# Turning the layer-normed rows by DMA transposes instead of TensorE in the first head of an attention-and-gate kernel

## The chip, the cores and the metric

The kernel runs on one core of one Trainium2 chip. The metric is the device time of the execution in microseconds (us), as the median of several runs.

## The reference

The kernel computes one block of attention with a gated feed-forward branch, in bfloat16. `x` is 2048 rows of 640, normalised per row without a learned scale. There are 32 heads of width 192 with a given key and value cache of 2048 rows, no mask. The feed-forward width F is 1536.

```python
x = A_x
xn = _layernorm(x, axis=-1)                      # (x - mean) / sqrt(var + 1e-5)
q = (xn @ wq).reshape(B, Sq, H, Dh).transpose(0, 2, 1, 3)
scores = jnp.einsum("bhqd,bhkd->bhqk", q, k_cache) * (Dh ** -0.5)
p = _softmax(scores, axis=-1)
o = jnp.einsum("bhqk,bhkd->bhqd", p, v_cache)
s = o.transpose(0, 2, 1, 3).reshape(B, Sq, H * Dh) @ wo
h = _silu(xn @ w1) * (xn @ w3)
return x + s * _silu(h @ w2)
```

## The kernel before

**Layout.** Everything that is multiplied by the weights needs the normalised rows with the 640 features on the partitions. This copy is `xnT`, 128 partitions x 5 chunks x 2048 rows. A second copy, `xnS`, holds the same with the upper and lower 64 partitions exchanged; `swap_rows(qb)` (L298 to L301) makes it for 512 rows with two DMAs from SBUF to SBUF, issued on GpSimd (POOL). Rows go by blocks of 512, `qb` = 0 to 3, and by tiles of 128, 0 to 15.

**Normalising.** `ln_stats(i)` (L179) takes mean and variance of a row tile on VectorE (DVE); for tiles 1 and 4 `ln_sums` does it on ScalarE (ACT). `ln_root(i0)` (L196) turns the variances of two tiles into 1/sqrt on ACT, `ln_scale(i0)` (L214) applies them on DVE. `ln_turn(i0)` (L224) then transposes the two tiles: ten transposes on TensorE (PE) into a PSUM tile of the pool `ps_st`, and two copies to `xnT` on ACT. That pool has two buffers, and the score tiles and the projections use the same two.

**A pair.** The attention of a head goes over four query blocks and, in each, over eight pairs of key tiles. `advance(hd, qb, p, extra)` (L432) does one pair: six score matmuls (L371), one exponential of 128x1024 on ACT (L377), and the value matmuls (L417) of a pair that was scored earlier. `extra` is more PE work, put behind the values. PE runs its instructions strictly in the order in which the program gives them (`pin` keeps that order on each engine).

**Head 0 is special.** While it runs, the rest of `x` is still being normalised, and head 0 and head 1 are projected block by block. `first_project(0, qb + 1)` projects the next block of head 0 (L277, ten matmuls), takes the maxima of the projected rows (L294) and makes the bound `nb` that the exponentials of that block need; `swap_rows(qb + 1)` follows, and `first_project(1, qb)` projects a block of head 1 (L283, twenty matmuls that read `xnT` and `xnS`). Later heads are projected one head ahead. What comes behind which pair is written out by hand in `at`, `extras` and `posts`:

```python
at = (1, 3, 4, 6) if qb else (3, 4, 5, 7)
extras = dict(zip(at, (steps((next_turn, 4 * qb + 4)), steps((next_turn, 4 * qb + 6)),
                       steps((first_project, 0, qb + 1)), steps((first_project, 1, qb)))))
```

so in block 0 the turns stand behind pairs 3 and 4 and the two projections behind pairs 5 and 7, and in blocks 1 and 2 behind pairs 1, 3, 4 and 6. In block 3 only `first_project(1, 3)` is left, behind pair 1.

**Keys.** `load_keys(h)` (L102) issues two DMA transposes (`KA`, `KB`) and the values `vt` on the queue of SyncE (SP). Keys have three buffers, so those of heads 0 to 2 wait for nothing. `copy_keys` (L116) makes a partly exchanged copy `KC` with two copies and a memset on POOL. `key_maxima` (L303) takes maxima of keys on DVE. Before the first pair, `first_bound` makes the bound of block 0 by way of a small matmul, with filler matmuls (`keep_busy`) around it.

After head 0 come 31 heads in the same manner, with feed-forward work between them, and then the output tiles. The change touches none of this.

Of the kernel before, what the change touches and what calls it, by code (L numbers as in the profile page):

```python
# [30 lines left out]
def _kernel_impl(ctx, tc, A_x, A_k_cache, A_v_cache, A_wq, A_wo, B_w1, B_w3, B_w2, out):  # L31
# [54 lines left out]
    def load_weights(h):  # L86
# [12 lines left out]
                keep(nc.gpsimd.dma_start(out=wq[ROWS[t], :, c0:c1], in_=w.rearrange("(s p) d -> p s d", p=DT)))  # L99
        return dict(wq=wq)  # L100

    def load_keys(h, mid=None):  # L102
        kh = A_k_cache[0, h]
        vh = A_v_cache[0, h]
        KA = kvp.tile([P, SK], BF16, tag="KA")
        KB = kvp.tile([P, SK], BF16, tag="KB")
        for K, c in ((KA, 0), (KB, DH - P)):
            for r in ((slice(0, HALF), slice(HALF, SK)) if h == 0 else (slice(0, SK),)):
                nc.sync.dma_start_transpose(out=K[:, r], in_=kh[r, c:c + P])  # L109
            if mid and K is KA:  # L110
                mid()
        vt = kvp.tile([P, NKT, DH + 2], BF16, tag="vt")
        nc.sync.dma_start(out=vt[:, :, 0:DH], in_=vh.rearrange("(t p) d -> p t d", p=P))
        return dict(KA=KA, KB=KB, vt=vt)

    def copy_keys(L, keep=pin):  # L116
        L["KC"] = KC = kvp.tile([P, HALF], BF16, tag="KC", name="KC")
# [10 lines left out]
    with ExitStack() as actx:  # L128
# [30 lines left out]
        x_all = lnx.tile([P, NQT, D], BF16, name="x_all")  # L159

        def load_x(eng, t0, t1):
            eng.dma_start(out=x_all[:, t0:t1, :], in_=x2[t0 * P:t1 * P, :].rearrange("(t p) d -> p t d", p=P))

        load_x(nc.sync, 0, 1)
        load_x(nc.scalar, 1, 2)
# [58 lines left out]
        def ln_turn(i0, copies=(nc.scalar.copy, nc.scalar.copy)):  # L224
            pst = ps_st.tile([P, 2, 1024], BF16, tag="st2", name="pst")
            for t, xn in enumerate(scaled.pop(i0)):
                for c in range(DC):
                    pin(nc.tensor.transpose(out=pst[:, t, c * P:(c + 1) * P], in_=xn[:, c * P:(c + 1) * P], identity=ident_bf[:]))
            return [lambda t=t, cp=cp: pin(cp(out=xnT[:, :, (i0 + t) * P:(i0 + t + 1) * P],
                                              in_=pst[:, t, 0:D].rearrange("p (c q) -> p c q", c=DC)))  # L230
                    for t, cp in enumerate(copies)]

        def next_turn(i0):
            for copy in ln_turn(i0):
                copy()

        keep_busy(15)
        ln_sums(1)
# [17 lines left out]
        def start_head(h):  # L256
            L = loads.pop(h)
            heads[h] = dict(
                h=h, L=L, vt=L["vt"],
                qA=qp.tile([P, SQ], BF16, tag="qA", name="qA"),  # L260
                qF=qfp.tile([P, SQ], BF16, tag="qF", name="qF"),
                qS=qp.tile([P, SQ], BF16, tag="qS", name="qS"),
                qD=qp.tile([DT, SQ], BF16, tag="qD", name="qD"),
                st=stt.tile([P, 4, NQB], F32, tag="st", name="st"),
            )
            pin(nc.vector.memset(heads[h]["st"][:], 0.0))
# [42 lines left out]
        def first_bound():  # L309
# [3 lines left out]
            pin(nc.vector.scalar_tensor_tensor(out=pr[:], in0=hd["st"][:, 0:2, 0], scalar=-SCALE * SLACK,  # L313
                                               in1=hd["st"][:, 2:4, 0], op0=ALU.mult, op1=ALU.mult))
            bp = ps_o.tile([P, 2, 512], F32, tag="ob0", name="bp")
            for t in range(2):
                pin(nc.tensor.matmul(bp[:, 0, 0:1], lhsT=ones_bf[:], rhs=pr[:, t:t + 1], start=(t == 0), stop=(t == 1)))
            nb = stt.tile([P, 1], F32, tag="nbb", name="nbb")
            pin(nc.vector.tensor_copy(out=nb[:], in_=bp[:, 0, 0:1]))
            hd["nb"] = [nb]  # L320
# [83 lines left out]
                late.append(rest)  # L404

        def values(hd, qb, p, pT2):
            vt = hd["vt"]
# [34 lines left out]
        start_head(0)  # L442
        loads[1] = load_weights(1)
        ln_sums(4)
        for s in range(2):
            for k in range(2):
                key_maxima(0, s, k, 2)
        maxima = project_chunk(0, 0, nc.scalar.copy)
        swap_rows(0)
        loads[1].update(load_keys(1))  # L450
        maxima()
        early = [scores(heads[0], 0, p) for p in range(2)]
        keep_busy(2)
        first_bound()
        keep_busy(4)
        ln_stats(5)
        warm = stt.tile([P, 1], F32, tag="warm", name="warm")
        pin(nc.gpsimd.partition_all_reduce(warm[:], heads[0]["nb"][0][:], P, bass_isa.ReduceOp.add))

        start_head(1)  # L460
        all_keys = [(s, k, NQB) for k in range(NQB) for s in range(2)]
        key_slots = list(all_keys)

        def first_project(h, qb):
            maxima = project_chunk(h, qb, nc.vector.tensor_copy if h == 0 else nc.scalar.copy)
            if h == 0:
                maxima()
                next_bound(qb)
            else:
                behind.append(maxima)  # L470

        def steps(*fs):
            return lambda: [f(*a) for f, *a in fs]

        posts = {
            (0, 1): ((ln_root, 4), (ln_stats, 6), (ln_scale, 4), (ln_stats, 7)),
            (0, 3): ((ln_root, 6), (ln_scale, 6), (ln_stats, 8), (ln_stats, 9)),
            (0, 5): ((ln_stats, 10), (ln_stats, 11), (ln_root, 8)),
            (0, 7): ((ln_scale, 8), (ln_root, 10)),
            (1, 2): ((ln_scale, 10), (ln_stats, 12), (ln_stats, 13)),  # L480
            (1, 5): ((ln_stats, 14), (ln_stats, 15), (ln_root, 12)),
            (1, 7): ((ln_scale, 12), (ln_root, 14)),
            (2, 2): ((ln_scale, 14),),
        }
        behind = []
        for qb in range(NQB):
            more = qb + 1 < NQB
            at = (1, 3, 4, 6) if qb else (3, 4, 5, 7)
            extras = dict(zip(at, (steps((next_turn, 4 * qb + 4)), steps((next_turn, 4 * qb + 6)),
                                   steps((first_project, 0, qb + 1)), steps((first_project, 1, qb)))))  # L490
            if not more:
                extras = {1: steps((first_project, 1, qb))}
                loads[2].update(load_weights(2))
                copy_keys(loads[2])
            for p in range(NPAIR):
                advance(heads[0], qb, p, extras.get(p), early.pop(0) if early else None)
# [310 lines left out]
```

## Time and profile before

| | |
|---|---|
| Time, median of 3 runs | 1957.43 us (1957.2 to 1957.73) |
| Span of the profiled execution | 1957.8 us |
| PE busy | 1941.8 us (99%) |
| ACT busy | 1219.9 us (62%) |
| DVE busy | 1137.9 us (58%) |
| POOL busy | 440.5 us (23%) |
| DMA, mean over the span | 78 GB/s |
| First score matmul of head 1 | 89.14 us |

The profiled execution's span, 1957.8 us, is its own time; it lies 0.35 us above the median of the runs. A busy share is that of the whole span. Head 0 with its preparation takes the first 89 us; a line of the timeline has the start and the length in us, engine, source line, operation, output<-input, shape, count, and in brackets the idle time of the engine before it and what ended it.

### The profile page before, as it was taken

Reading aid. Unit: us, or ns where it says so; the run is one execution under the profiler, and the core shown is the slowest. Engines: PE = TensorE matmul, PEld = TensorE weight load, DVE = VectorE, ACT = ScalarE, POOL = GpSimd, SP = SyncE. Lnnn points to the kernel's source line nnn. Section 1 sums busy time; section 2 is a strip of 40 time slices with the busy share of each in tenths; the row PEclk is TensorE's granted clock in tenths of the full one; section 3 lists DMA queues with packets and bytes.
Section 4 is the critical chain, followed back from the end, with each engine's and each line's share of the span. In section 5 each row is a group of like instructions: output and inputs, shape, how many; then the busy total and the mean of one; then the engine's idle time right before and its main releaser. Section 6 shows DMA issues by size and latency. Waiting matters only on the chain.

```text
span 1957.8 us, 60489 instructions
## 1 busy us (share of the span) xinstructions
PE 1941.8 (99%) x27236; PEld 1332.9 (68%) x27236; DVE 1137.9 (58%) x2258; ACT 1219.9 (62%) x1192; POOL 440.5 (23%) x640
## 2 busy tenths in 40 slices
PE   8999999999999999999999999999999999999998
PEld 4676666667766666666666666666666666667776
DVE  6665657676666666666666666666665654531111
ACT  6777767776777777777777777777777777210000
POOL 3422222222222222222222222222222220000000
PEclk8999999999999999999999999999999999999999
DMA  9421313222233332232323232323232112837882
GB/s 183 104 66 42 74 44 74 53 69 59 60 68 63 68 62 68 54 90 68 76 54 76 54 76 46 84 46 84 46 75 44 44 50 75 261 77 139 156 152 56
DMA packets 352906, 153.52 MB, mean 78 GB/s; under 512 B 303792, under 2 KB 345744, under 8 KB 352640
## 3 DMA queue, kind: packets, MB, share of 16 engines
q1 hardware_dynamic: 337200, 117.82, 28.4%
q0 software_dynamic: 8800, 26.55, 5.7%
q10 hardware_dynamic: 6640, 5.21, 1.2%
q8 instruction: 215, 3.52, 0.8%
q14 instruction: 51, 0.42, 0.1%
HBM read 56.23 MB, written 31.98 MB: 45 GB/s over the span
## 4 chain that ended last, share of the span: by engine, by line
PE 97%; DVE 1%; DMA 1%; ACT 0%; POOL 0%; SPq 0%; issue 0%; POOLq 0%; DVEq 0%
PE obank L417 34%; PE st L371 33%; PE ps L283 14%; PE ps_s L630 11%; PE ps_f L649 3%; PE ps_gu L536 2%; DMA KB<-in_A_k_cache_dram 0%; PE ps L277 0%; DMA xnS<-xnT 0%; ACT pT L377 0%; SPq L109 0%; DVE u L541 0%; PE fill L177 0%; ACT t L539 0%; DVE a L543 0%
## 5 line engine op out<-in xcount | busy, mean ns | idle before, releaser
L377 ACT ACTIVATE pT<-st,nb 128x1024 bf16<-128x1024 f32 x1016 | 1130.6, 1114 | 439.8 <-PE st L371 439.1
L417 PEld LDWEIGHTS <-pT 64*128 64x128 bf16 x16384 | 720.9, 94 | 236.1 <-DVE osum L388 0.9
L417 PE MATMUL obank<-vt,pT 64*128 64x193 bf16 x16384 | 856.7, 243 | 0.4 <-DVE osum L388 0.4
L387 DVE COPY osum<-obank 128x386 f32<-128x386 f32 x256 | 142.4, 556 | 513.3 <-PE obank L417 513.3
L371 PE MATMUL st<-qA,KA 64*128 64x512 bf16 x2048 | 394.6, 377 | 3.0 <-ACT pT L377 1.1
L371 PE MATMUL st<-qD,KC 64*128 64x512 bf16 x1024 | 385.6, 377 | 1.9 <-issue 1.8
L371 PE MATMUL st<-qS,KB 64*128 64x512 bf16 x1024 | 385.5, 377 | 0.6 <-POOL qS L289 0.6
L371 PE MATMUL st<-qS,KC 64*128 64x512 bf16 x1024 | 385.6, 377 | 0.1
L371 PE MATMUL st<-qF,KB 64*128 64x512 bf16 x1024 | 385.7, 377 | 0.0
L289 POOL COPY qS<-qA 64x512 bf16<-64x512 bf16 x256 | 193.3, 755 | 598.7 <-DVE qA L285 590.3
L283 PE MATMUL ps<-xnT,wq 64*128 64x512 bf16 x1240 | 288.4, 376 | 0.0
L283 PE MATMUL ps<-xnS,wq 64*128 64x512 bf16 x1240 | 285.9, 376 | 0.1
L371 PEld LDWEIGHTS <-KC 64*128 64x128 bf16 x2048 | 192.1, 94 | 118.3 <-issue 2.0
L630 PE MATMUL ps_s<-wo_sb,oT 128*128 128x320 bf16 (+2 forms) x1536 | 208.8, 299 | 0.0
L371 PEld LDWEIGHTS <-KB 64*128 64x128 bf16 x2048 | 192.8, 94 | 17.8 <-issue 2.9
L283 PEld LDWEIGHTS <-wq 64*128 64x128 bf16 x2480 | 123.7, 94 | 114.0 <-issue 0.4
L630 PEld LDWEIGHTS <-oT 128*128 128x128 bf16 x1536 | 148.3, 98 | 60.5
L394 DVE TENSOR_TENSOR ostage<-osum,rl_all 128x384 bf16<-128x384 f32 x256 | 150.5, 588 | 8.8
L388 DVE TENSOR_TENSOR osum<-osum,obank 128x386 f32<-128x386 f32 x256 | 142.6, 557 | 8.9
L371 PEld LDWEIGHTS <-KA 64*128 64x128 bf16 x2048 | 106.2, 94 | 22.3 <-issue 7.4
L635 DVE SCALAR_TENSOR_TENSOR tmp<-ps_s,g_all 128x320 f32<-128x320 f32 (+2 forms) x32 | 15.6, 487 | 175.8 <-PE ps_s L630 175.8
L99 POOL DMA_DIRECT2D wq<-in_A_wq_dram x62 | 45.5, 733 | 278.0 <-PE ps L283 265.8
(86 smaller groups left out, 1228.4 us busy)
## 6 DMA issues: line engine op xcount, KB each, us to landing
vt<-in_A_v_cache_dram SPq DMA_DIRECT2D x32, 768.0 KB, 6.2
o_scr<-ostage SPq DMA_DIRECT2D x64, 384.0 KB, 3.2
wo_sb<-in_A_wo_dram POOLq DMA_DIRECT2D x1, 7680.0 KB, 32.1
wq<-in_A_wq_dram POOLq DMA_DIRECT2D x31, 160.0 KB, 3.0
hT_scr<-hblk SPq DMA_DIRECT2D x16, 256.0 KB, 2.9
xnS<-xnT POOLq DMA_DIRECT2D x8, 320.0 KB, 6.6
xt<-in_A_x_dram POOLq DMA_DIRECT2D x16, 160.0 KB, 9.2
wq<-in_B_w_dram POOLq DMA_DIRECT2D x31, 80.0 KB, 2.5
```

The costliest lines, as they stand in the source:

```text
L99: keep(nc.gpsimd.dma_start(out=wq[ROWS[t], :, c0:c1], in_=w.rearrange("(s p) d -> p s d", p=DT)))
L283: pin(nc.tensor.matmul(ps[:, t * 512:(t + 1) * 512], lhsT=wq[ROWS[t], s, :], rhs=xs[ROWS[t], s // 2, qs], start=(s == 0), stop=(s == 2 * D ...
L289: keep(nc.gpsimd.tensor_copy(out=qS[ROWS[t], qs], in_=qA[ROWS[1 - t], qs]))
L371: pin(nc.tensor.matmul(st2[:, t * 512:(t + 1) * 512], lhsT=k[ROWS[t], ks], rhs=q[ROWS[t], qs], start=(s == 0), stop=(s == 2)))
L377: pin(nc.scalar.activation(out=pT2[:], in_=st2[:], func=ACT.Exp, scale=SCALE, bias=nb[:]))
L387: pin(nc.vector.tensor_copy(out=osum[:], in_=ov[:, 0, :, 0:DH + 1]))
L388: pin(nc.vector.tensor_tensor(out=osum[:], in0=osum[:], in1=ov[:, 1, :, 0:DH + 1], op=ALU.add))
L394: pin(nc.vector.tensor_tensor(out=ostage[:, b * 2:b * 2 + 2, hg * DH:(hg + 1) * DH], in0=osum[:, :, 0:DH], in1=rl.unsqueeze(2).to_broadcas ...
L417: pin(nc.tensor.matmul(acc["o"][b][:, r, (j % 2) * 256:(j % 2) * 256 + DH + 1], lhsT=pT2[ROWS[r], t * 512 + j * P:t * 512 + (j + 1) * P], ...
L536: pin(nc.tensor.matmul(ps[:, o:o + 512], lhsT=w_sb[:, c, fl * P:(fl + 1) * P], rhs=xnT[:, c, qs], start=(c == 0), stop=(c == DC - 1)))
L630: pin(nc.tensor.matmul(ps, lhsT=oT[:, k, :], rhs=wo_sb[:, k, c0:c1], start=(k == 0), stop=(k == OC - 1)))
L649: pin(nc.tensor.matmul(ps[:, pi * 512:pi * 512 + c1 - c0], lhsT=hT[:, fc, qsl], rhs=w2_sb[:, fc, c0:c1], start=(fc == 0), stop=(fc == FC - ...
```

## The change

Rows 0 to 511 are turned as before. For the other twelve row tiles, `ln_send(i0)` takes the place of `ln_turn`: it scales two tiles and issues one DMA transpose for each on SP, from the scaled tile in SBUF to `xnT`. The statistics, roots, scalings and transposes of the second block (tiles 4 to 7) are placed ahead of the first pair; those of blocks 2 and 3 follow in `posts`. `first_project(0, qb + 1)` stands behind pair 3 and `first_project(1, qb)` behind pair 6 in blocks 0 to 2, and `swap_rows` behind pair 4. The loads of head 1's and head 2's keys on SP come behind the transposes that precede them in program order; `copy_keys` of heads 1 and 2 moves to blocks 2 and 3. The maxima of head 1's projected rows (`behind`) are taken behind pair 3 of block 2 and pairs 3, 5 and 7 of block 3; before, the fourth of them was never taken. The loads of `x` keep their program order.

```diff
+    def load_key(L, h, name):
+        keep = pin if h <= 2 else (lambda x: x)
+        L[name] = K = kvp.tile([P, SK], BF16, tag=name, name=name)
+        c = {"KA": 0, "KB": DH - P}[name]
+        for r in ((slice(0, HALF), slice(HALF, SK)) if h == 0 else (slice(0, SK),)):
+            keep(nc.sync.dma_start_transpose(out=K[:, r], in_=A_k_cache[0, h, r, c:c + P]))
+
+    def load_values(L, h):
...
-        def next_turn(i0):
-            for copy in ln_turn(i0):
-                copy()
+        def ln_send(i0):
+            ln_scale(i0)
+            for t, xn in enumerate(scaled.pop(i0)):
+                pin(nc.sync.dma_start_transpose(out=xnT[:, :, (i0 + t) * P:(i0 + t + 1) * P], in_=xn[:]))
...
         ln_sums(4)
-        for s in range(2):
-            for k in range(2):
-                key_maxima(0, s, k, 2)
+        for k in range(2):
+            key_maxima(0, 0, k, 2)
+        ln_stats(5)
+        ln_stats(6)
+        ln_root(4)
+        for k in range(2):
+            key_maxima(0, 1, k, 2)
         maxima = project_chunk(0, 0, nc.scalar.copy)
         swap_rows(0)
-        loads[1].update(load_keys(1))
         maxima()
+        pr = first_product()
+        ln_stats(7)
+        ln_root(6)
+        ln_send(4)
+        ln_send(6)
+        load_key(loads[1], 1, "KA")
         early = [scores(heads[0], 0, p) for p in range(2)]
         keep_busy(2)
-        first_bound()
+        first_bound(pr)
         keep_busy(4)
-        ln_stats(5)
...
         posts = {
-            (0, 1): ((ln_root, 4), (ln_stats, 6), (ln_scale, 4), (ln_stats, 7)),
-            (0, 3): ((ln_root, 6), (ln_scale, 6), (ln_stats, 8), (ln_stats, 9)),
-            (0, 5): ((ln_stats, 10), (ln_stats, 11), (ln_root, 8)),
-            (0, 7): ((ln_scale, 8), (ln_root, 10)),
-            (1, 2): ((ln_scale, 10), (ln_stats, 12), (ln_stats, 13)),
-            (1, 5): ((ln_stats, 14), (ln_stats, 15), (ln_root, 12)),
-            (1, 7): ((ln_scale, 12), (ln_root, 14)),
-            (2, 2): ((ln_scale, 14),),
+            (0, 1): ((ln_stats, 8),),
+            (0, 2): ((ln_stats, 9),),
+            (0, 4): ((ln_stats, 10), (ln_root, 8)),
+            (0, 5): ((ln_stats, 11), (ln_send, 8), (ln_root, 10)),
+            (0, 6): ((ln_send, 10),),
+            (0, 7): ((load_key, loads[1], 1, "KB"), (load_values, loads[1], 1)),
+            (1, 1): ((ln_stats, 12),),
+            (1, 2): ((ln_stats, 13),),
+            (1, 4): ((ln_stats, 14), (ln_root, 12)),
+            (1, 5): ((ln_stats, 15), (ln_send, 12), (ln_root, 14)),
+            (1, 6): ((ln_send, 14),),
         }
         behind = []
         for qb in range(NQB):
             more = qb + 1 < NQB
-            at = (1, 3, 4, 6) if qb else (3, 4, 5, 7)
-            extras = dict(zip(at, (steps((next_turn, 4 * qb + 4)), steps((next_turn, 4 * qb + 6)),
-                                   steps((first_project, 0, qb + 1)), steps((first_project, 1, qb)))))
+            extras = {3: steps((first_project, 0, qb + 1)), 6: steps((first_project, 1, qb))}
             if not more:
                 extras = {1: steps((first_project, 1, qb))}
                 loads[2].update(load_weights(2))
-                copy_keys(loads[2])
             for p in range(NPAIR):
                 advance(heads[0], qb, p, extras.get(p), early.pop(0) if early else None)
-                if p == 3 and behind:
+                if behind and (qb, p) in ((2, 3), (3, 3), (3, 5), (3, 7)):
                     behind.pop(0)()
-                if p == (4 if qb else 5) and more:
+                if p == 4 and more:
                     swap_rows(qb + 1)
-                if p == 6 and qb == 0:
+                if p == 3 and qb == 2:
                     copy_keys(heads[1]["L"])
                     loads[2] = load_keys(2)
+                if p == 5 and not more:
+                    copy_keys(loads[2])
```

More of the change, by code (lines that the diff above doesn't have):

```diff
@@ L100, in load_weights @@
         return dict(wq=wq)
-    def load_keys(h, mid=None):
[L103 to L114, printed above, removed]
+    def load_key(L, h, name):
[5 more added lines that the diff above has]
+    def load_values(L, h):
+        keep = pin if h <= 2 else (lambda x: x)
+        L["vt"] = vt = kvp.tile([P, NKT, DH + 2], BF16, tag="vt", name="vt")
+        keep(nc.sync.dma_start(out=vt[:, :, 0:DH], in_=A_v_cache[0, h].rearrange("(t p) d -> p t d", p=P)))
+    def load_keys(h, mid=None):
+        L = {}
+        load_key(L, h, "KA")
+        if mid:
+            mid()
+        load_key(L, h, "KB")
+        load_values(L, h)
+        return L
     def copy_keys(L, keep=pin):
@@ L161, in load_x @@
         def load_x(eng, t0, t1):
-            eng.dma_start(out=x_all[:, t0:t1, :], in_=x2[t0 * P:t1 * P, :].rearrange("(t p) d -> p t d", p=P))
+            pin(eng.dma_start(out=x_all[:, t0:t1, :], in_=x2[t0 * P:t1 * P, :].rearrange("(t p) d -> p t d", p=P)))
         load_x(nc.sync, 0, 1)
@@ L258, in start_head @@
             heads[h] = dict(
-                h=h, L=L, vt=L["vt"],
+                h=h, L=L,
                 qA=qp.tile([P, SQ], BF16, tag="qA", name="qA"),
@@ L307, in key_maxima, with first_product @@
                                         apply_absolute_value=True))
-        def first_bound():
+        def first_product():
             hd = heads[0]
@@ L314, in first_bound @@
                                                in1=hd["st"][:, 2:4, 0], op0=ALU.mult, op1=ALU.mult))
+            return pr
+        def first_bound(pr):
+            hd = heads[0]
             bp = ps_o.tile([P, 2, 512], F32, tag="ob0", name="bp")
@@ L406, in values @@
         def values(hd, qb, p, pT2):
-            vt = hd["vt"]
+            vt = hd["L"]["vt"]
             def part(ts, bs):
@@ L444, in _kernel_impl @@
         ln_sums(4)
-        for s in range(2):
-            for k in range(2):
-                key_maxima(0, s, k, 2)
+        for k in range(2):
[5 more added lines that the diff above has]
+            key_maxima(0, 1, k, 2)
         maxima = project_chunk(0, 0, nc.scalar.copy)
         swap_rows(0)
-        loads[1].update(load_keys(1))
         maxima()
+        pr = first_product()
[4 more added lines that the diff above has]
+        load_key(loads[1], 1, "KA")
         early = [scores(heads[0], 0, p) for p in range(2)]
         keep_busy(2)
-        first_bound()
+        first_bound(pr)
         keep_busy(4)
-        ln_stats(5)
         warm = stt.tile([P, 1], F32, tag="warm", name="warm")
         pin(nc.gpsimd.partition_all_reduce(warm[:], heads[0]["nb"][0][:], P, bass_isa.ReduceOp.add))
-        start_head(1)
         all_keys = [(s, k, NQB) for k in range(NQB) for s in range(2)]
@@ L464, in first_project @@
         def first_project(h, qb):
+            if h == 1 and 1 not in heads:
+                start_head(1)
             maxima = project_chunk(h, qb, nc.vector.tensor_copy if h == 0 else nc.scalar.copy)
```

## The prediction

> **What bounds the kernel now.** I read the page first: TensorE is busy 99% of the span and makes 97% of the chain that ended last, so only time in which PE waits, or work taken off PE, can move the end. I read the chain next, then the PE timeline, because the change touches only the first 90 us (head 0).
>
> ```profile
> PE   8999999999999999999999999999999999999998
> ...
> PE 97%; DVE 1%; DMA 1%; ACT 0%; POOL 0%; SPq 0%; issue 0%; POOLq 0%; DVEq 0%
> ```
>
> From the PE timeline, first the price of a pair with nothing beside it, then the places where head 0 costs more:
>
> ```profile
> 85.20 0.38 PE L371 MATMUL st<-qA,KA 64*128 64x512 bf16 x1
> ...
> 86.51 0.38 PE L371 MATMUL st<-qA,KA 64*128 64x512 bf16 x1
> ```
>
> One pair (six score and sixteen value matmuls) starts 1.31 us after the last.
>
> ```profile
> 26.47 0.73 PE L228 MATMUL pst<-ident_bf,xn 128*128 128x128 bf16 x10
> ...
> 31.69 2.32 PE L277 MATMUL ps<-xnT,wq 128*128 128x512 bf16 x10
> ...
> 38.01 0.37 PE L371 MATMUL st<-qD,KC 64*128 64x512 bf16 x1 [1.81 <-issue]
> ...
> 49.93 2.33 PE L277 MATMUL ps<-xnT,wq 128*128 128x512 bf16 x10
> ...
> 67.51 2.33 PE L277 MATMUL ps<-xnT,wq 128*128 128x512 bf16 x10
> ```
>
> From 49.93 to 67.51 is 17.58 us. The work in it without the turn is 8 pairs, a head-0 projection (2.26) and a head-1 projection (2.16): 8 x 1.315 + 4.42 = 14.94. The two turns cost 2.64, or 1.32 each: 0.73 of transposes and about 0.6 of PE waiting for a PSUM tile and for the copies on ACT. One more stall, 1.81 us, is put down to "issue".
>
> Last, the DMA answers, asked for the stretches in which each transfer was issued. The first is the start (two lines), the second a steady head, the third the last swap.
>
> ```profile
> xnS<-xnT POOLq DMA_DIRECT2D x1, 320.0 KB, 16.2
> KA<-in_A_k_cache_dram SPq DMA_TRANSPOSE x1, 22.5
> ```
> ```profile
> KA<-in_A_k_cache_dram SPq DMA_TRANSPOSE x1, 5.0
> ```
> ```profile
> xnS<-xnT POOLq DMA_DIRECT2D x1, 320.0 KB, 3.6
> ```
>
> The last number is us from issue to landing. A DMA transpose and the SBUF-to-SBUF swap that take 5.0 and 3.6 us apart take 22.5 and 16.2 together. The packet records show why the two belong together: from 24 to 36 us a 256-byte transpose row takes about 190 ns, against 18 ns elsewhere, while the swap's 4 KB pieces trickle.
>
> **What goes.** Before, from 26.47 (where pair 3's extra work starts) to head 1's first scores at 89.14 is 62.67 us. The work left after the change is 28 pairs x 1.315 = 36.8, three head-0 projections x 2.26 = 6.8, four head-1 projections x 2.16 = 8.6: 52.2. So at most **10.4 us** can go: six turns (about 8.1), the 1.81 stall, and a wait of 0.45 for xnS at 78.96. The twelve ACT copies (0.64 each) go too; ACT isn't the bound, so their price is already in the turns. The order of the built program agrees: 60 transposes fewer on PE, twelve transposing DMAs more on SP.
>
> The 1.81 stall I take as gone. PE has then issued about 256 matmuls with their weight loads, an instruction transfer is on the DMA queues at 35.6, and KA and KB of head 1 are still crawling; after the change KB is issued a whole block later.
>
> **Ahead of attention.** DVE idles 2.26 us before KB's maxima; the statistics of tiles 5 and 6 (1.07 each) go there, shift those maxima by some 0.4 us, and still end before the maxima of qA (16.47, set by ACT's cast). Tile 7's statistics (1.07) and four scalings (0.4 each) fill 18.55 to 21.2, inside the 3.46 us in which DVE waited for bp before 22.01. On ACT two roots (0.7 and 0.5) fit ahead of the casts at 15.85 and of the first exponential at 22.20. I cost this at nothing; its cover is those waits, and beyond them each us would be a us of PE.
>
> **The DMA transposes of rows 512 to 1023.** Ready at 20.05, 20.4, 20.8 and 21.2, issued on SP (free at 15.3), ahead of KA of head 1. The first projection of block 1 is now behind pair 3, so PE wants them at 26.47: some 5.3 us after the last is ready. What is queued behind it on PE is everything, PE being in order. No row shows a transpose out of SBUF. From below: alone, 128x2048 lands in 5.0 us, so four of 128x640 (1.25 times as much) would be there at about 26.5, wait 0. From above: beside the swap, KA took 22.5. The swap of block 0 is issued at 18.98, unchanged, and landed at 35.2; the four transposes now take KA's place next to it. I take the near row, KA in this very place: landing at 36, **+9.5**. A PE idle for 9.5 us also loses clock. The windows view shows it after the gaps of about 1 us each at 10 to 16 us:
>
> ```profile
> 15.00:20.00 5.00, 3.51 (x12) 0.82 (x12) 2.85 (x5) 1.07 (x2) 4.88 (x8) 0.50 1.12 326
> 20.00:25.00 5.00, 5.00 (x36) 1.86 (x34) 2.22 (x9) 2.75 (x6) 0.34 (x1) 0.61 1.23 121
> 25.00:30.00 5.00, 4.19 (x68) 2.97 (x63) 2.75 (x8) 4.74 (x7) 0.40 (x1) 1.00 1.25 91
> ```
>
> The granted clock (seventh column) stays at 0.5 for some us into dense work. Four to five us at half clock: **+2.3** (0 to 5).
>
> [...]
>
> **Blocks 2 and 3.** Counted from a projection's start T: casts, maxima and bound keep DVE to T+5.5, two statistics and four scalings to T+8.9, SP issues (0.6 each) to T+9.6, landing, at a guess from the half-size KA transposes (5.1), 4.5 later at T+14.1. Needed at T+14.95. But the swap of the block before is issued at T+6.2 (POOL, after nb) and lands at T+11.4, so its tail overlaps. KA of head 2 after the second swap's tail (its rows start near 44, run free from 46) lost some 1.7 us: 0.8 late, twice, **+1.6** (0 to 8).
>
> **The last swap.** Its queue on POOL gains copy_keys of head 1 (1.03 + 1.04 + 0.16 = 2.3 us by L118 to L120) between nb and the swap. Before, xnS landed 11.4 us after block 3's projection started; now 13.7, wanted at 12.3 (one pair more lies between): **+1.4**. Keys of heads 1 and 2 move on SP to behind the sends; they have 10 us and more in hand, nothing. Maxima of head 1 move to the last block: DVE ends near 89.1 where it ended at 86.6, against 90.2 for the first exponential of head 1; nothing, but the cover is 1 us.
>
> **Sum.** -10.4 + 9.5 + 2.3 + 1.6 + 1.4 = +4.4 on the profiled execution's 1957.8 (the median shown, 1957.43, lies 0.35 lower): 1961.8, say 1962. Rivals are given against the median too.
>
> **Rivals.** *No convoy (faster).* The transposes reach the rings after 22 us, not at 20 as KA did, and the swap drains ahead of them, or rows out of SBUF don't clash with it. Then wait and clock go: -10.4 + 1.6 + 1.4, about 1950. For it: KA after the second swap lost under 2 us. Against: the first swap's pieces hardly moved before 26 us. It decides from a wait of 5.5 us: landing before 32 means faster.
> *Half a convoy.* Landing near 30: 3.5 + 1 us of wait and clock, 1954.5.
> *Slow at every block.* Rows out of SBUF cost what KA cost beside the swap, 22.5 / 16 = 1.4 us per 128x128 square: 20 squares take 28 us, three times over, some 62 us more, 2020. Against: KA alone, 0.31 per square. [...]
>
> **Chances.** Convoy at the first block 0.45 (its own range 1958 to 1966), no convoy 0.27, half a convoy 0.20, slow everywhere 0.08. The range 1949 to 1968 leaves out the last case, the upper tail of the first and the lower of the second. This kernel's measurement tells about 0.2% (3.9 us) from no change. Faster by more: 0.27 + 0.09 of the half case = 0.36. Slower by more: 0.36 of the convoy and 0.08 = 0.44. Within: 0.20.
>
> **What would show it.** Right: a PE gap of 8 to 11 us near 27, ended by DMA xnT<-xn; the granted clock at 0.5 behind it; L277 at about 36, 53 to 55 and 70; a wait for xnS near 1.4 us; no 1.81 "issue". Wrong: L277 near 26.5 with no gap (no convoy), or gaps above 15 us at all three projections (slow everywhere). The steady heads must keep 12.67 us per block; if they don't, the whole working is off.

## The result and the profile after

The changed kernel takes 1963.63 us (median of 6 runs, 1960.19 to 1964.62), the kernel before 1957.32 beside it: ratio 1.003, 95% interval 1.002 to 1.0041. It is slower by about 6 us; 1962.0 was forecast. The profiled execution of the changed kernel has a span of 1961.9 us and a time of 1963.84. In every run below the time is 1.7 to 2.1 us above the span. The span of before, 1957.8, is therefore not a time: it belongs to an execution of some 1959.7 us (an estimate from that offset), about 2 us slower than the median. The prediction took it for a time; as it happens to lie near the median of 1957.3, the base of the forecast was sound all the same.

The page after, the lines that answer to those of before, and the last of them as it was in the page of before (L417 there is L429 here):

```profile
PE   7999999999999999999999999999999999999998
...
PE 96%; DVE 1%; DMA 1%; SPq 0%; POOL 0%; ACT 0%; issue 0%; POOLq 0%; DVEq 0%
...
L429 PE MATMUL obank<-vt,pT 64*128 64x193 bf16 x16384 | 861.9, 243 | 3.8 <-DVE osum L400 3.6
```
```profile
L417 PE MATMUL obank<-vt,pT 64*128 64x193 bf16 x16384 | 856.7, 243 | 0.4 <-DVE osum L388 0.4
```

PE is still the chain. Its first slice fell from 8 to 7 tenths, and the value matmuls, which waited 0.4 us for the eviction of their PSUM banks in the whole kernel before, now wait 3.6. (The eviction is DVE's move of a finished block's sums out of PSUM, to `osum`; the next block's value matmuls wait for it, here for up to 1.42 us.) The PE timeline of the changed kernel (start, length, engine, line, operation; in brackets the idle time before it and what ended it) has both losses:

```profile
22.12 0.51 PE L429 MATMUL obank<-vt,pT 64*128 64x193 bf16 x8 [0.21 <-ACT pT L389]
...
30.90 4.26 PE L285 MATMUL ps<-xnT,wq 128*128 128x512 bf16 x10 [5.99 <-DMA xnT<-xn]
...
41.83 0.39 PE L383 MATMUL st<-qA,KA 64*128 64x512 bf16 x2 [0.45 <-ACT pT L389]
...
46.31 0.34 PE L429 MATMUL obank<-vt,pT 64*128 64x193 bf16 x4 [0.36 <-DVE osum L400]
48.07 0.34 PE L429 MATMUL obank<-vt,pT 64*128 64x193 bf16 x4 [1.42 <-DVE osum L400]
...
52.31 2.33 PE L285 MATMUL ps<-xnT,wq 128*128 128x512 bf16 x10
...
65.78 0.34 PE L429 MATMUL obank<-vt,pT 64*128 64x193 bf16 x4 [0.36 <-DVE osum L400]
67.55 0.34 PE L429 MATMUL obank<-vt,pT 64*128 64x193 bf16 x4 [1.42 <-DVE osum L400]
...
70.12 2.33 PE L285 MATMUL ps<-xnT,wq 128*128 128x512 bf16 x10
...
83.45 0.39 PE L291 MATMUL ps<-xnS,wq 64*128 64x512 bf16 x2 [0.63 <-DMA xnS<-xnT]
```

PE reaches the projection of block 1 at 24.91 and starts it at 30.90; it then takes 4.26 us instead of 2.26. The projections of blocks 2 and 3 start without a wait. At the start of blocks 1 and 2 stands a new pair of waits, 0.36 and 1.42, for DVE's eviction; at block 3, where a projection still stands behind pair 1, there is none. The 1.81 us of "issue" is gone. It is gone in the run pe1 below as well (0.16 at most), where PE turns rows again; why it stood there before stays open.

The windows view (seventh column: granted clock) shows what the waits do to the clock:

```profile
25.00:30.00 5.00, 0.00 (x0) 0.00 (x0) 0.00 (x0) 0.74 (x1) 0.40 (x1) 0.81 1.17 143
30.00:35.00 5.00, 4.10 (x10) 1.31 (x10) 0.00 (x0) 0.00 (x0) 0.00 (x0) 0.51 0.51 91
...
45.00:50.00 5.00, 3.22 (x38) 1.90 (x36) 4.75 (x12) 2.07 (x3) 0.00 (x0) 0.85 0.93 111
50.00:55.00 5.00, 5.00 (x38) 2.40 (x36) 1.12 (x4) 1.78 (x2) 0.00 (x0) 0.81 1.11 244
```

By the trace's record of the granted clock it is at half from 28.05 to 34.88 and again from 48.53 to 51.94, behind the first pair of eviction waits. The DMA answers: issues from 17 to 27 us, then SP's transposes by themselves (first line: issue time on SP in ns, least, median and most).

```profile
xnS<-xnT POOLq DMA_DIRECT2D x2, 320.0 KB, 7.7
xnT<-xn SPq DMA_TRANSPOSE x4, 7.0
```
```profile
L243 SPq DMA_TRANSPOSE xnT<-xn x4: 1462/2092/2580, 19.3 to 26.0; - x4
...
DMA to landing us min/median/max: 4.9/7.0/9.0
```

The swap, which took 16.2 us beside KA, takes 7.7 beside the transposes; there was no convoy. SP spends 8.5 us in issuing four transposes, and the last, issued at 25.95, lands 4.86 us later.

From PE ready (24.91) to head 1's first scores (93.63) the stretch is 68.72 us, against 62.67 before: +6.05, which is the whole loss in the medians. The spans differ by only 4.1 chiefly because the preparation in the profiled execution of before was 1.5 us longer (first value matmul at 23.63, here at 22.12).

### The profile page after: what moved, and what is told of

It is laid out like the page before. It is cut to its first block, busy times and chain, and to the rows that moved or that the text cites. A ratio compares the mean times of both kernels' runs of the same rounds, so it can differ in the third digit from the quotient of the medians.

```text
span 1961.9 us, 60406 instructions
## 1 busy us (share of the span) xinstructions
PE 1938.5 (99%) x27176; PEld 1348.4 (69%) x27176; DVE 1137.3 (58%) x2260; ACT 1213.7 (62%) x1180; POOL 441.2 (22%) x640
## 4 chain that ended last, share of the span: by engine, by line
PE 96%; DVE 1%; DMA 1%; SPq 0%; POOL 0%; ACT 0%; issue 0%; POOLq 0%; DVEq 0%
PE obank L429 34%; PE st L383 33%; PE ps L291 13%; PE ps_s L653 11%; PE ps_f L672 3%; PE ps_gu L559 2%; PE ps L285 0%; DMA KB<-in_A_k_cache_dram 0%; DMA xnT<-xn 0%; DVE st L190 0%; DMA xnS<-xnT 0%; DVE st L302 0%; SPq L107 0%; SPq L243 0%; DVE u L564 0%
## 5 line engine op out<-in xcount | busy, mean ns | idle before, releaser
L429 PEld LDWEIGHTS <-pT 64*128 64x128 bf16 x16384 | 730.1, 94 | 231.4 <-DVE osum L400 3.3
L429 PE MATMUL obank<-vt,pT 64*128 64x193 bf16 x16384 | 861.9, 243 | 3.8 <-DVE osum L400 3.6
L383 PE MATMUL st<-qA,KA 64*128 64x512 bf16 x2048 | 399.1, 377 | 2.8 <-DVE a L566 1.0
L291 PEld LDWEIGHTS <-wq 64*128 64x128 bf16 x2480 | 128.3, 94 | 110.5 <-issue 1.1
L383 PEld LDWEIGHTS <-KA 64*128 64x128 bf16 x2048 | 110.3, 94 | 21.3 <-issue 7.6
## 6 DMA issues: line engine op xcount, KB each, us to landing
wo_sb<-in_A_wo_dram POOLq DMA_DIRECT2D x1, 7680.0 KB, 33.1
```

What stands on the lines that cost most here:

```text
L291: pin(nc.tensor.matmul(ps[:, t * 512:(t + 1) * 512], lhsT=wq[ROWS[t], s, :], rhs=xs[ROWS[t], s // 2, qs], start=(s == 0), stop=(s == 2 * D ...
L383: pin(nc.tensor.matmul(st2[:, t * 512:(t + 1) * 512], lhsT=k[ROWS[t], ks], rhs=q[ROWS[t], qs], start=(s == 0), stop=(s == 2)))
```

## The experiments

All times are medians; the ratio is to runs of the kernel before on the same chip beside them (medians 1956.36 to 1957.32). The stretch runs from the first value matmul of head 0 to the first projection matmul of head 2, so it leaves the preparation out. The last column counts windows of half clock (3.41 us each) in it. The last three columns are of one profiled execution each; that of cover_swap_late took 2.4 us more than the median of its run, that of late5_roots 2.3, so there the stretch is no measure of the median. The run two_queues, 1968.90 us, stands in the text alone, since its first value matmul itself came 13 us late.

| Run | us | ratio to before, 95% | stretch | first projection of block 1 starts (wait) | half |
|---|---|---|---|---|---|
| before | 1957.32 | | 67.81 | 31.69 (0) | 0 |
| changed kernel | 1963.63 | 1.0030 (1.0020 to 1.0041) | 73.80 | 30.90 (5.99) | 3 |
| cover | 1958.67 | 1.0009 (1.0000 to 1.0018) | 68.89 | 31.00 (5.67) | 2 |
| cover_swap_late | 1957.91 | 1.0009 (1.0000 to 1.0018) | 71.21 | 28.01 (4.01) | 2 |
| late5 | 1962.36 | 1.0025 (1.0013 to 1.0037) | 73.39 | 30.47 (3.26) | 2 |
| pe1 | 1961.73 | 1.0032 (1.0020 to 1.0044) | 70.65 | 30.17 (0) | 1 |
| pe1_cover | 1954.40 | 0.9986 (0.9977 to 0.9995) | 63.85 | 31.00 (0) | 0 |
| late_swap | 1952.40 | 0.9972 (0.9962 to 0.9982) | 62.40 | 27.06 (0) | 0 |
| x_late | 1956.97 | 0.9994 (0.9983 to 1.0006) | 67.51 | 28.10 (3.64) | 1 |
| late_swap2 | 1951.51 | 0.9964 (0.9952 to 0.9975) | 61.50 | 27.96 (0.34) | 0 |
| pe1_cover2 | 1955.93 | 0.9996 (0.9983 to 1.0008) | 65.86 | 29.90 (0) | 1 |
| late5_roots | 1959.13 | 1.0003 (0.9992 to 1.0015) | 71.79 | 30.84 (4.10) | 3 |
| swap_mid | 1953.89 | 0.9984 (0.9974 to 0.9994) | 65.66 | 27.89 (3.80) | 1 |

**cover: a projection behind pair 1 again.**

```diff
-            extras = {3: steps((first_project, 0, qb + 1)), 6: steps((first_project, 1, qb))}
-            if not more:
-                extras = {1: steps((first_project, 1, qb))}
+            extras = {3: steps((first_project, 0, qb + 1))}
+            if qb:
+                extras[1] = steps((first_project, 1, qb - 1))
+            if not more:
+                extras[3] = steps((first_project, 1, qb))
```

> One edit on the changed kernel: head 1's projection of block q moves from behind pair 6 of block q to behind pair 1 of block q+1 (block 3's own to behind pair 3). Theory, uncovered eviction: in the changed kernel nothing but score and value matmuls follows the start of a block, so PE waits for DVE's eviction of the last block's PV banks (0.36 and 1.42 us, at blocks 1 and 2: 3.56), for ACT once behind each early head-1 projection (0.45 twice) and for xnS (0.6 to 1.0), and the 1.42 in block 1 is followed by a half-clock window that costs about 1.7. With a projection in that place all these go: 5 to 7 us less than the changed kernel, about 1957 to 1959, and the waits on osum fall under 0.3 us each. The wait of 6.0 for the DMA transposes in block 0 stays. Rival, the lost time is all in block 0's wait and its clock: within 1.5 us of the changed kernel, 1962 to 1965, because the waits come back in another place (a PSUM tile, the bound of head 1 late by a us or more).

5.0 us less than the changed kernel in the medians and in the spans (1956.9), 4.1 by the ratios: the lower edge of what was expected, or just under it. The PE timeline of cover no longer has a wait for osum:

```profile
31.00 0.58 PE L285 MATMUL ps<-xnT,wq 128*128 128x512 bf16 x1 [5.67 <-DMA xnT<-xn]
...
42.10 0.51 PE L429 MATMUL obank<-vt,pT 64*128 64x193 bf16 x8 [0.76 <-ACT pT L389]
...
49.62 2.33 PE L285 MATMUL ps<-xnT,wq 128*128 128x512 bf16 x9
...
58.62 0.51 PE L429 MATMUL obank<-vt,pT 64*128 64x193 bf16 x8 [1.31 <-ACT pT L389]
```

So 4 to 5 of the 6 us lost come back without touching a DMA transpose: the removed turns had been a cover, that is, work on PE during which a wait ran out unseen. Part of it returns as waits for ACT, 0.76 and 1.31.

**cover_swap_late: cover, with the swap of block 0 issued behind block 1's casts.**

```diff
         maxima = project_chunk(0, 0, nc.scalar.copy)
-        swap_rows(0)
...
                 if p == 4 and more:
+                    if qb == 0:
+                        swap_rows(0)
                     swap_rows(qb + 1)
```

> The kernel of the run cover, with one more edit: the SBUF-to-SBUF swap of block 0 is issued behind block 1's casts instead of at 19 us, so that no copy on the software queue runs beside the four DMA transposes of rows 512 to 1023. Theory of the convoy (the swap's packets hold the transposes up, or its being ahead in the rings does): the transposes land 3 us earlier or more, the first projection of block 1 starts at 27.5 or sooner where it started at 30.9, and the time falls by 3 to 5 us against the run cover. Rival, SP's issue: the four transposes are issued one after another in 8.5 us, the last at about 26, whatever else runs, and land 4.5 to 5 us after: the projection starts at 30.5 to 31 as before and the time is within 1 us of the run cover.

From the PE timeline of cover_swap_late:

```profile
28.01 3.39 PE L285 MATMUL ps<-xnT,wq 128*128 128x512 bf16 x9 [4.01 <-DMA xnT<-xn]
...
49.22 4.00 PE L285 MATMUL ps<-xnT,wq 128*128 128x512 bf16 x9 [3.14 <-DMA xnT<-xn]
```

The transposes land 3.0 us earlier, short of the "27.5 or sooner" and far from "as before": with the swap out of the rings (the DMA queues, with what they still hold of earlier transfers) they issue in 6.2 us instead of 8.0. The time hardly moves, 0.8 us in the medians and nothing by the ratios: in the profiled execution two swaps in a row then meet block 2's transposes (PE waits 3.14 us at 49.22, and the clock halves). The swap does hold the transposes up, by 3 us.

**x_late: cover, with x's rows 1024 to 2047 loaded behind the four sends.**

```diff
-        load_x(nc.sync, 8, 12)
-        load_x(nc.sync, 12, 16)
...
         ln_send(6)
+        load_x(nc.sync, 8, 12)
+        load_x(nc.sync, 12, 16)
         load_key(loads[1], 1, "KA")
```

> The kernel of the run cover, with one edit: the loads of rows 1024 to 2047 of x (two of 640 KB, whose 1280-byte packets keep SP's rings until 22 us) are issued on SP behind the four DMA transposes of block 1 instead of at the start. Theory of the order on the rings: the transposes' rows now begin near 20, ahead of the swap's packets instead of behind them, and the two crawl together, as KA and the swap did in the kernel before and in pe1 (21 to 22 us to landing): landing at 33 or later, the first projection of block 1 later than the 31.0 of cover, and 2 to 8 us slower than cover. Rival, the rings were simply full: with the loads out of the way the rows are there 2 to 3 us sooner, the projection starts near 28 to 29 and the time is 2 to 4 us less than cover. Rival, SP's issue: the start stays at 30.5 to 31.

The projection starts at 28.10, and the time is 1.7 us below cover in the medians, 2.9 by the ratios. The packet records show the order: the swap's 4 KB pieces run from 19 to 22 us at 39 to 49 per us, the transposes' rows follow from 21 at a median of 18 ns each. The rival of full rings has its earlier start, though cover_swap_late had put the 3 us down to the swap alone: taking away either tenant, the x loads or the swap, lets the four land at 28. That full rings are the reason no view shows. What is left is SP's issue, four times 1.2 us at least (7.5 us in all here).

**swap_mid: cover, with the swap issued at 23.5 us.**

```diff
-        swap_rows(0)
...
         pin(nc.gpsimd.partition_all_reduce(warm[:], heads[0]["nb"][0][:], P, bass_isa.ReduceOp.add))
+        swap_rows(0)
```

> The kernel of the run cover, with one edit: the swap of block 0 is issued on POOL behind the all-reduce at 24 to 25 us, so that its packets come while the rows of the four SBUF-sourced transposes are already running (they begin at 20 without the swap, and landed at 28.0 in cover_swap_late). In the kernel before and in pe1 KA's rows, from DRAM, ran first and the swap came 2 us later, and both crawled for 12 us. Theory, the order alone decides: the same crawl here, rows of some 190 ns, landing at 32 or later, the swap 10 us and more to landing, the time 2 to 8 us above cover. Rival, the kind decides (only transposes that read DRAM crawl beside the swap): rows stay at 18 ns, landing at 28 to 29.5, the swap within 8 us, and the time 0 to 3 us below cover.

The projection starts at 27.89; the time is 4.8 us below cover, more than the 3 allowed for. In the profiled executions the stretch is 3.2 us shorter, with one half-clock window behind the wait where cover has two, and the preparation, at full clock here and at half from 16 to 23 us in cover, is 1.0 us shorter. The DMA answer for issues from 15 to 34 us, swap_mid first, then pe1:

```profile
xnS<-xnT POOLq DMA_DIRECT2D x2, 320.0 KB, 9.5
...
xnT<-xn SPq DMA_TRANSPOSE x4, 5.6
KA<-in_A_k_cache_dram SPq DMA_TRANSPOSE x1, 13.6
```
```profile
xnS<-xnT POOLq DMA_DIRECT2D x2, 320.0 KB, 16.5
...
KA<-in_A_k_cache_dram SPq DMA_TRANSPOSE x1, 21.3
```

KA, which reads DRAM, crawls with the swap in both (13.6 and 21.3 us to landing); the SBUF-sourced transposes don't (5.6). The proof has a gap: the swap's packets came at 27 us here, when the transposes' rows were through, so the two did not run together. Where they did (block 2 of cover_swap_late, 39 to 46 us), the swaps moved up to 62 pieces per us and the rows' median, us by us, was 18 to 32 ns; in pe1, from 23 to 28 us, the swap moved 4 to 10 and the rows' median went up to 195. The four of cover_swap_late were held up all the same: one issue took SP 4.9 us, and the first needed 10.4 us to landing. That the source decides whether both crawl is likely, not shown.

**late5: block 1's projection behind pair 5, and late5_roots: the same, with statistics 10 and 11 a pair earlier.**

```diff
-            extras = {3: steps((first_project, 0, qb + 1)), 6: steps((first_project, 1, qb))}
+            extras = dict(zip((3, 6) if qb else (5, 7), (steps((first_project, 0, qb + 1)), steps((first_project, 1, qb)))))
...
-                if p == 4 and more:
+                if p == (4 if qb else 6) and more:
```

> One edit on the changed kernel: in block 0 the projection of block 1 moves from behind pair 3 to behind pair 5, and head 1's from behind pair 6 to behind pair 7 (and the next swap behind pair 6). PE then has two more pairs, 2.6 us, ahead of the wait for the DMA transposes, which land at 30.8. Theory, landing is set by SP and the rings and not by PE: the wait falls from 6.0 to about 3.4, the half-clock window after it stays or shrinks: 2 to 4 us less than the changed kernel, 1960 to 1962; the bound and the swapped rows of block 1 may cost up to 1.5 of it at the start of block 1, since they are ready 5.6 us and more after the projection starts. Rival: the transposes land later because PE, ACT and DVE traffic goes on beside them; then the wait stays at 5 to 6 and the time within 1 us of the changed kernel.

> The kernel of the run late5, with the statistics of tiles 10 and 11 a pair earlier, so that the root of tiles 10 and 11 on ACT no longer stands ahead of an exponential while it waits for statistics queued behind block 1's casts (PE lost 2.94 us to that in late5). Theory: two pairs more ahead of the wait for the DMA transposes are worth what they take off that wait (2.7), so 2 to 4 us less than the changed kernel, about 1960, and about 3 less than late5. Rival, the freed time goes into the swap or the evictions at block 1: the same as late5, 1962.

late5's wait is 3.26, as the first theory has it, but the time is only about 1 us better than that of the changed kernel (ratio 1.0025 against 1.003). The timeline of late5, ACT and PE:

```profile
38.56 0.29 ACT L214 ACTIVATE lv<-mv,eps_t 128x2 f32<-128x2 f32 x1 [10.35 <-DVE mv L191]
...
40.14 0.37 PE L291 MATMUL ps<-xnT,wq 64*128 64x512 bf16 x1 [2.94 <-ACT pT L389]
```

The root of tiles 10 and 11 stands ahead of an exponential on ACT and waits for statistics that are queued on DVE behind block 1's casts and maxima; PE pays 2.94 us. In late5_roots that wait is gone and 3.2 us with it in the medians, as expected, though its wait for the transposes is 4.10, PE having come earlier. So a statistic put behind a projection was not free here (2.94 us), although DVE is busy for 58% of the span.

**pe1: rows 512 to 1023 back on TensorE, the next swap behind pair 6.**

```diff
-        ln_send(4)
-        ln_send(6)
+        ln_scale(4)
+        ln_scale(6)
...
+            if qb == 0:
+                extras = {3: steps((turn_now, 4)), 4: steps((turn_now, 6)), 5: steps((first_project, 0, 1)),
+                          7: steps((first_project, 1, 0))}
...
```

> One part of the change undone: rows 512 to 1023 are turned on TensorE again (two turns, behind pairs 3 and 4 of block 0, the projection of block 1 behind pair 5, head 1's behind pair 7); rows 1024 to 2047 stay with the DMA transposes. Theory: block 0 loses its wait of 6.0 and the half clock behind it (2.0), pays two turns (2.64): about 5.4 us less than the changed kernel, 1958; the evict waits of blocks 1 and 2 stay. A rival by which it was the instruction stream that stalled PE (the 1.81 of issue in the kernel before, which is gone in the changed one) gives that back: 1960. If the DMA transposes of block 1 had cost nothing, it would be slower than the changed kernel, 1966.

A miss: 5.4 us less than the changed kernel was expected; the ratios show no gain (1.0032 against 1.003), the medians 1.9 us. The wait of 6 went, the turns came, and ACT's root cost 2.39 us, as in late5; the eviction waits stayed, with a window of half clock behind the one of block 2. By itself the run does not tell what the first block's transposes cost.

**two_queues: cover_swap_late, with tiles 6 and 7 sent from ACT.**

```diff
-        ln_send(6)
+        ln_send(6, nc.scalar)
```

> The kernel of the run cover_swap_late, with one edit: the transposes of tiles 6 and 7 are issued by ACT, those of tiles 4 and 5 by SP, so that the four are no longer issued one after another on one engine. Theory, what is left of the wait there (4.0 us, start at 28.0) is SP's serial issue (6.2 us for four): the landing comes 2 us earlier or more, the first projection of block 1 at 26 or sooner, while ACT's two issues of 1.2 to 2.5 us each put off the first exponentials and give PE back up to 3 us of that ahead of the projection. Rival, the rate of the rows on the rings sets it: the start stays at 28 and the time is up to 3 us more than cover_swap_late, from ACT.

1968.9 us, ratio 1.0058 (1.0045 to 1.007): neither theory. From the timeline of two_queues:

```profile
20.10 2.56 SPq L243 DMA_TRANSPOSE xnT<-xn  x2
...
25.91 8.45 ACTq L243 DMA_TRANSPOSE xnT<-xn  x2
28.60 2.19 SPq L107 DMA_TRANSPOSE KA<-in_A_k_cache_dram  x1
34.41 2.12 ACT L389 ACTIVATE pT<-st,nbb 128x1024 bf16<-128x1024 f32 x2 [14.08 <-issue]
```

ACT's first transpose starts at 25.91, when SP's rows are through (at 25); SP's KA starts at 28.60, when ACT's first has landed (2.7 us after its issue), and ACT's second at 33.1, when KA has landed (4.5); behind it the first exponentials come after 14.08 us of idle ACT. So the transposes of the two queues ran one behind another here, with semaphore instructions at their line (L243) on both queues; what would happen without them no run shows. A second queue buys nothing here.

**pe1_cover and late_swap: both repairs together.** pe1_cover is cover, turns for rows 512 to 1023, the projection behind pair 5, earlier statistics and KA behind block 2's sends. late_swap has the last three too and keeps all twelve DMA transposes; its two swaps wait for the landing of block 1's. The lines of late_swap on the swaps:

```diff
...
                 if p == 4 and more:
                     swap_rows(qb + 1)
+                    if qb == 0:
+                        swap_rows(0)
```

> The head-1 projections of the run cover, with rows 512 to 1023 turned on TensorE (two turns behind pairs 3 and 4 of block 0, the projection of block 1 behind pair 5), rows 1024 to 2047 by DMA transposes; the statistics of tiles 10 and 11 a pair earlier, so that no root on ACT waits behind the casts of block 1 as in pe1 and late5; KA of head 1 issued behind the sends of block 2. Theory: what is lost in the changed kernel is the DMA transposes of the first block (wait 6.0, clock 2.0) and the uncovered evictions; without both, the first 90 us cost the 52.2 us of work plus two turns (2.6) and about 2 us of ACT waits seen in cover, 57 against 62.7 in the kernel before: 5 to 6 us faster than that, about 1951. Rival: each cover gives its time back in another wait; then it is within 2 us of the kernel before or of cover.

> All twelve DMA transposes kept, on top of cover: the projection of block 1 behind pair 5 of block 0, and both swaps of blocks 0 and 1 issued on POOL only once block 1's transposes have landed; KA of head 1 behind the sends of block 2; statistics of tiles 10 and 11 a pair earlier. Theory, landing at 28.0 without the swap and PE ready two pairs later, near 26.6: a wait of 1.4, too short to lose the clock, and block 2's transposes no longer beside the swaps: 52.2 + 1.4 + about 2 of ACT waits, 55.6 against 62.7, so 6 to 7 us faster than the kernel before, about 1950. Rival: two swaps in a row hold up block 2's transposes as in cover_swap_late (a wait of 3.1 and 1.7 of clock there): about 1955.

Both beat the kernel before, by 2.7 and 4.7 us, and fall short of their forecasts by 3.4 and 2.4. From the PE timelines of pe1_cover and late_swap:

```profile
45.60 2.32 PE L289 MATMUL ps<-xnT,wq 128*128 128x512 bf16 x9 [2.13 <-DMA xnT<-xn]
```
```profile
36.40 0.39 PE L291 MATMUL ps<-xnS,wq 64*128 64x512 bf16 x2 [1.43 <-DMA xnS<-xnT]
```

Most of what is missing are waits for the next DMA: pe1_cover waits 2.13 us for block 2's transposes, late_swap 1.43 for xnS and 1.25 for block 3's transposes. late_swap is 2.0 us better; two turns would be 2.6.

**late_swap2 and pe1_cover2: the waits that were left.** In late_swap2, against late_swap (each half of a swap can now be issued by itself):

```diff
-            extras = {3: steps((first_project, 0, qb + 1))}
+            extras = {4 if qb == 2 else 3: steps((first_project, 0, qb + 1))}
...
-                    swap_rows(qb + 1)
                     if qb == 0:
+                        swap_rows(1, (0,))
                         swap_rows(0)
+                        swap_rows(1, (1,))
+                    else:
+                        swap_rows(qb + 1)
```

In pe1_cover2, against pe1_cover, it is `4 if qb == 1 else 3`, and nothing else.

> The kernel of the run late_swap, with the two waits left in its trace attacked: the swap of block 0 is issued between the two halves of the swap of block 1 (it had been last of the four, and PE waited 1.43 us for it), and the projection of block 3 goes from behind pair 3 to behind pair 4 of block 2 (PE waited 1.25 us for its DMA transposes there). Theory, each wait on PE moves the end by its length: 2 to 2.7 us less than late_swap, about 1950. Rival, they return as a later wait (block 3's bound or swap, head 1's bound): the same as late_swap.

> The kernel of the run pe1_cover (rows 512 to 1023 on TensorE) with its one long wait attacked, 2.13 us for the DMA transposes of block 2: the projection of block 2 goes from behind pair 3 to behind pair 4 of block 1. Theory: the wait falls by the 1.3 us of a pair, 1.3 us less than pe1_cover, about 1953; it stays 2 to 3 us above late_swap2, because two turns on TensorE (2.6) remain. Rival, landing shifts with it or the bound of block 2 is late: the same as pe1_cover.

The first was half right, the second wrong. The PE timeline of late_swap2:

```profile
27.96 2.32 PE L285 MATMUL ps<-xnT,wq 128*128 128x512 bf16 x10 [0.34 <-ACT rstd L217]
...
42.18 2.32 PE L285 MATMUL ps<-xnT,wq 128*128 128x512 bf16 x10 [1.60 <-DMA xnT<-xn]
...
51.16 0.51 PE L429 MATMUL obank<-vt,pT 64*128 64x193 bf16 x8 [1.31 <-ACT pT L389]
...
60.00 2.33 PE L285 MATMUL ps<-xnT,wq 128*128 128x512 bf16 x10
```

The waits of 1.43 and 1.25 went and 1.60 for block 2's transposes came: 0.9 us less, which the intervals don't tell from nothing. In pe1_cover2 the wait for the transposes turned into 1.08 and 2.62 for roots and exponentials on ACT, with a window of half clock behind the second, and nothing was won. late_swap2, at 1951.51, is the best version: 0.9964 of the kernel before.

## Why the prediction was right in its number and wrong in its steps

The prediction's own signs were met in part: the clock at half behind a gap that DMA xnT<-xn ended, and no "issue" stall; but the gap was 6.0 us and not 8 to 11, the projection of block 1 started at 30.9 and not at 36, and the wait for xnS was 0.6 and not 1.4.

**What goes (-10.4): right.** Turns, "issue" stall and the wait of 0.45 are gone. late_swap2 shows that the gain was real: 6.3 of the 10.4 us come out of its stretch.

**First block's DMA transposes (+9.5): mechanism wrong, size 6.0.** "KA in this very place" was the step that failed. The row reads DRAM and ran ahead of the swap; the transposes ran behind it, at 18 ns a row in the median. (Nor did every row beside the swap take about 190 ns in the kernel before, as the working has it: of the rows from 24 to 36 us 18% took over 100 ns, and the median is 18.) The condition of the rival "no convoy", that the swap drains ahead of them, was met, but not its result: landing in time. The bound from below, 26.5, left out SP: four issues of 1.46 to 2.58 us (0.6 is what the working took at blocks 2 and 3), with packets of the x loads running until 22.9 us and those of the swap until 25.6. That an issue can take long stood in the SP timeline of before, where one transpose behind the x loads held SP for 8.90 us:

```profile
15.33 8.90 SPq L109 DMA_TRANSPOSE KA<-in_A_k_cache_dram  x1
```

Landing at 30.8 is close to what the rival "half a convoy" had (near 30), at a chance of 0.20, and its time was 1954.5. The wait of 6.0 lies just over the named break-even of 5.5. That the kernel is 6 us slower, and not the fraction of one that this would give, has the next reason.

**A term that was missing: the cover behind pair 1 (+3.6, and the clock behind it).** The working counted the turns as pure cost. The trace of before held the sign, in the waits for osum behind the turns:

```profile
45.64 1.01 PE L417 MATMUL obank<-vt,pT 64*128 64x193 bf16 x20 [0.16 <-DVE osum L388]
...
63.22 1.01 PE L417 MATMUL obank<-vt,pT 64*128 64x193 bf16 x20 [0.26 <-DVE osum L388]
```

Without work behind pair 1 they are 1.78 per block, twice, one of them followed by a window of half clock (half of 3.41 us, some 1.7), and 0.45 for ACT twice: 6.2 together. The run cover took 4 to 5 of it back.

**Clock (+2.3): right,** 2.0 at the first projection; the second drop belongs to the term above.

**Blocks 2 and 3 (+1.6): 0,** but only because PE came 6 us late to block 2, 21.4 us after the start of block 1's projection instead of 14.95. Where PE was in time (pe1_cover), the transposes landed 14.6 us after the start of block 1's projection, forecast 14.1, and PE waited 2.1.

**The last swap (+1.4): 0.8.** It landed 13.3 us after block 3's projection started, forecast 13.7; the scores behind the projection that waits for it start 2.97 us after that projection instead of 2.16.

**Ahead of attention, key loads, head 1's maxima (0): right** in the changed kernel, as far as the medians tell (the time rose by 6.3 us, the stretch by 6.0); the roots on ACT became a cost of 2.4 to 2.9 us as soon as the projection moved (late5, pe1).

Sum over the stretch from PE ready to head 1's first scores: 52.2 of work + 6.0 + 2.0 + 3.6 + 1.7 + 0.9 + 0.8 = 67.2 against 68.7 measured; 1.5 us of small waits are not assigned. The prediction's terms make 52.2 + 9.5 + 2.3 + 1.6 + 1.4 = 67.0, so the 1.7 us between the sums is all but 0.1 of the miss in the time (1963.63 against 1961.8). That the number came out is luck: 6.0 us too much on the transposes, the clock and the swap stood for 6.2 us of uncovered waits that nobody had counted. With the prediction's own terms at the sizes measured, -10.4 + 6.0 + 2.0 + 0 + 0.8, the kernel would have become 1.6 us faster, not slower.

## What to carry to other kernels

Before work is taken off the engine that sets the time, look at which waits stand right behind that work. Small waits for an eviction or an exponential there can be the sign of a cover: here 0.16 and 0.26 us for the eviction became 1.78 per block without the turns. Price the removal at the wait without the cover. Price a new transfer by its own issues and by what is still moving when it is issued: here four issues took SP 8.5 us and the last landed 4.86 us after its issue, where KA in the same place had taken 22.5 us and was no bound. Moving the consumer of the transfer back by two pairs, and the swap that ran beside it behind its landing, took away a wait of 5.67 us (late_swap, which also moves KA, against cover).

## What the hardware showed that was not expected

One DMA transpose of 128x640 out of SBUF held SP for 1.2 us where the swap came later (1215 to 1243 ns for rows 512 to 1023 in swap_mid), for 1.46 to 2.58 us in the changed kernel, for up to 2.9 in pe1 and in one case for 4.9 (block 2 of cover_swap_late). The shortest time from the start of the issue to landing was 2.6 us (late_swap, late_swap2, x_late).

A short stall cost the clock at some places and not at others. The pair of waits of some 0.36 and 1.42 us, with 0.34 us of matmuls between them, stands at eight places in the changed kernel, late5, late5_roots and pe1; at three of them, one each in the changed kernel (48.53), late5_roots and pe1, a window of half clock followed. Single waits of up to 2.39 us in head 0 (pe1; 1.60 in late_swap2, 2.13 in pe1_cover) brought none, all those of 2.62 (pe1_cover2) and more brought one or more. So single waits of 2.62 to 3.3 us were enough and, at times, 1.8 us of waiting inside 2.1; what decides at the pairs is not shown. Every half-clock stretch in the traces of the two kernels is a multiple of 3.41 us long (10.24 in the kernel before; 3.41, 6.83 and 3.41 in the changed kernel), but for the one at the end of each (3.96 and 4.11).
